# Attention with a soft mixture of experts on one core: local products over 128 keys instead of 64, paced transfers, four PSUM tiles for the output

## The chip, the cores and the metric

The kernel runs on one core of a Trainium2 chip. Its time is the device time of one execution, in microseconds (us), and the kernel before was run three times: 454.8, 461.24 and 464.32 us, median 461.24 us. The engines of the core work in parallel, each on its own queue of instructions in order: TensorE (PE; its weight loads stand as PEld), VectorE (DVE), ScalarE (ACT), GpSimd (POOL) and SyncE (SP), which here issues the transfers (DMA) between device memory and SBUF. Matrix products land in PSUM, eight banks of 512 fp32 values per partition.

## The reference

Eight batches of eight heads, 576 positions, head width 64; then a soft mixture of eight experts with four slots each over all 4608 tokens:

```python
scores = (q @ k.T) / sqrt(64), causal;  a = softmax(scores);  local = a @ v
q_p = phi(q)                                   # elu(x) + 1
mem_out = (q_p @ M_prev) / (q_p @ z_prev + 1e-6)
x = g * mem_out + (1 - g) * local              # g = sigmoid(beta), per head
logits = x @ phi                               # 4608 x 32
d = softmax over the tokens;  slot_input = d.T @ x
h = relu(slot_input[e] @ w1[e]);  slot_out[e] = h @ w2[e]      # 512 -> 1024 -> 512
c = softmax over the slots;  result = c @ slot_out
```

All of it is fp32. An fp32 product stands in the profile as two matmuls with a weight load each; the scores use three fp32r products of split operands.

## The kernel before, in words

**Units.** The attention is cut in 32 units `n` (a batch and a pair of heads; the two heads `h` lie on partitions 0 to 63 and 64 to 127). In a unit the last 512 queries are four blocks `i` of 128 queries, which see the first 192, 320, 448 and 576 keys. The first 64 queries of all units are done apart, in 16 small units ("a" operations). Nine groups `g` of tokens then run through the dispatch softmax ("x" operations), with a running maximum.

**Steps of a unit.** `ldq` and `ldv` load q and k, and v with `M` and `z`; `qhi`, `qlo`, `khi`, `klo` split q and k (POOL); `s` makes scores in PSUM (L367, L376); `mx` masks them and takes the row minimum (DVE, L394); `ex` takes the exponential (ACT, L401); `t` transposes the probabilities in blocks of 64 keys x 128 (two heads side by side; L404) and `te` copies them to SBUF (L283 on ACT, L286 on DVE); `av` multiplies with v (L433); `m` multiplies phi(q) with `M` and `z` (L442) into the same PSUM tile; `dn`, `mu`, `ad` normalise and add (L447, L454, L471). Each product of `av` is over 64 keys of one head for 64 queries, so TensorE works as four tiles of 64x64, and block `i` takes 8i+10 products (88 per unit). `pace` and its tiny copies do not exist yet.

**Order.** `SEQ` is a written table of some 2100 operations; `pin` ties every engine's instructions to that order. The digit behind a colon picks which of four PSUM tiles (two banks each) an operation gets. `EV` says which engine does a copy. `WORD` says where each of the 64 weight tiles of 512 KB is kept: with '' in space of its own, otherwise in a buffer that is free by then. Weight tiles that `WORD` does not hold are loaded in the last phase over used ones.

**Last phase.** `f1`, `f1t`, `f2` are the experts' layers. `comb(dh, g)` makes the output of a group, half the columns at a time: twice two products of 32 slots (L874) into a PSUM tile of two banks (three such tiles rotate), ACT scaling one pair (L880), DVE the other (L877), then a store of 512 KB.

Of the kernel before, what the change touches and what calls it, by code (L numbers as in the profile page):

```python
# [20 lines left out]
VM = 585 + 65  # L21
AU = 256 + 130 + 130
CW = 256 + S + 64
# [3 lines left out]
gate@0 la@0 la@1 ldq@1 ldv@1 as@0:0 ap1@0 aexp@0:1 amx.0@0 amx.1@0 aex.0@0 aphi@0 aex.1@0 at@0:1 as@1:0 ate@0 amx.0@1  # L27
aav@0:1 amx.1@1 am@0 aex.0@1 qhi@0 qp1@0 khi@0 la@2 adn@0 aex.1@1 qlo@0 qexp@0:0 klo@0 at@1:2 ate@1 amu@0 qhi@1 qphi@0
qp1@1 s.2@0:1 khi@1 qlo@1 aad@0 qexp@1:0 s.3@0:2 klo@1 mx.2.1@0 ldq@2 s.10@0:3 qphi@1 ex.2.1@0 ap1@1 mx.3a.1@0 s.2@1:0
mx.1.0@0 mx.3b.1@0 ex.1.0@0 mx.0.1@0 ldq@3 mx.1.1@0 ex.3.1@0 mx.0.0@0 ex.0.1@0 mx.3a.0@0 s.3@1:3 ex.0.0@0 ex.1.1@0  # L30
qhi@2 mx.2.0@1 aexp@1:2 khi@2 mx.3a.1@1 ex.2.0@1 qlo@2 aphi@1 mx.3b.1@1 t.C@0:2 mx.3a.0@1 ex.3.1@1 mx.3b.0@0 te.CX@0
s.10@1:3 klo@2 mx.3b.0@1 mx.2.1@1 te.CY@0 mx.2.0@0 ex.3.0@1 aav@1:0 am@1 as@2:2 mx.0.1@1 ex.2.1@1 qhi@3 av.1@0:1 la@3
amx.0@2 mx.1.0@1 aex.0@2 khi@3 ex.0.1@1 m.0@0 mx.1.1@1 ex.1.0@1 av.0@0 mx.0.0@1 qlo@3 ex.1.1@1 amx.1@2 s.10@2:3 dn.0@0
ex.0.0@1 aex.1@2 adn@1 ex.2.0@0 mu.0@0 at@2:2 klo@3 ex.3.0@0 amu@1 t.C@1:1 ate@2 mx.0.1@2 t.B@0:2 mx.1.0@2 ad.0@0
te.CY@1 mx.0.0@2 s.10@3:0 mx.1.1@2 te.BX@0 aad@1 te.CX@1 te.BY@0 t.A@0:3 ap1@2 mx.0.1@3 aexp@2:2 s.2@2:1 mx.1.0@3
te.AY@0 aphi@2 mx.0.0@3 te.AX@0 s.3@2:2 mx.1.1@3 mx.2.1@2 av.2@0:0 mx.3a.1@2 w@0 m.1@0 mx.3a.0@2 aav@2:3 am@2 av.3@0
qp1@2 mx.3b.1@2 mx.3b.0@2 la@4 adn@2 ap1@3 qexp@2:2 mx.2.0@2 amu@2 as@3:1 ldq@4 ldv@2 dn.1@0 av.1@1:3 aad@2 amx.0@3
mu.1@0 aex.0@3 m.0@1 av.0@1 amx.1@3 ex.1.0@2 ad.1@0 qphi@2 ex.0.0@2 t.B@1:1 aexp@3:0 dn.0@1 ex.0.1@2 x3.0@0:2 ex.1.1@2
mu.0@1 te.BX@1 aphi@3 te.BY@1 t.C@2:3 ad.0@1 x3e.0@0 aex.1@3 t.A@1:0 ex.2.1@2 qhi@4 te.CX@2 at@3:2 te.CY@2 s.2@3:1
khi@4 te.AX@1 te.AY@1 qlo@4 ate@3 ex.3.1@2 s.3@3:3 mx.2.1@3 ex.3.0@2 w@1 av.2@1:2 mx.2.0@3 ex.2.0@2 klo@4 mx.3a.1@3  # L40
m.1@1 aav@3:0 mx.3a.0@3 am@3 av.3@1 la@5 qp1@3 mx.3b.1@3 adn@3 ap1@4 mx.3b.0@3 qexp@3:3 amu@3 as@4:1 ldv@3 dn.1@1
av.1@2:0 aad@3 ldq@5 amx.0@4 amx.1@4 aex.0@4 mu.1@1 aexp@4:1 m.0@2 aex.1@4 av.0@2 aphi@4 ex.1.0@3 ad.1@1 qphi@3 at@4:1
# [36 lines left out]
mx.0.0@11 te.AY@9 qlo@12 s.3@11:1 mx.2.0@11 ex.2.1@10 av.2@9:3 ex.3.0@10 mx.2.1@11 klo@12 mx.3a.1@11 m.1@9 aav@11:2
mx.3a.0@11 am@11 av.3@9 la@13 qp1@11 mx.3b.1@11 adn@11 ap1@12 mx.3b.0@11 qexp@11:1 amu@11 as@12:0 ldv@11 dn.1@9  # L80
av.1@10:2 aad@11 ldq@13 amx.0@12 mu.1@9 aex.0@12 m.0@10 av.0@10 amx.1@12 ex.0.0@11 ad.1@9 qphi@11 ex.1.0@11 x4@1:0
aexp@12:3 dn.0@10 ex.0.1@11 aphi@12 aex.1@12 ex.1.1@11 mu.0@10 at@12:3 t.B@10:1 ex.2.0@11 x4a@1 ad.0@10 ate@12
t.C@11:2 w@11 ex.3.1@11 te.BX@10 s.10@12:3 te.BY@10 te.CX@11 t.A@10:0 qhi@13 te.CY@11 mx.1.0@12 s.2@12:1 khi@13
ex.2.1@11 mx.0.1@12 mx.1.1@12 te.AY@10 qlo@13 mx.0.0@12 s.3@12:2 te.AX@10 mx.2.0@12 ex.3.0@11 x3.1@2:3 mx.2.1@12
# [148 lines left out]
def tile_attn_soft_moe(ctx, tc, qk, vm, au, beta, phi, w1, w2, cst, out):  # L233
# [21 lines left out]
    psD = tc.alloc_tile_pool(name="psD", bufs=1, space=PSUM)  # L255
    ATT = (psD,)

    mk = fix.tile([128, 1152], F32, name="mk")
    maskq, mask2 = mk[:, 0:S], mk[:, S:S + 64]
    ph = fix.tile([128, NP, 32], F32, name="ph")  # L260
    gt = fix.tile([128, NP, 2, 4], F32, name="gt")
# [715 lines left out]
```

## Time and profile before

| what | value |
|---|---|
| median of three runs | 461.24 us (454.8 to 464.32) |
| the profiled execution | 462.31 us, of which span 460.4 us |
| busy: PE, DVE, ACT, POOL | 376.2, 308.9, 278.5, 198.3 us |
| attention with pipeline full, 22 to 386 us | PE 301.3 of 364 us |
| last phase, 398 to 460 us | 62 us |

Busy time is the union of an engine's instructions; TensorE's are pipelined, so its busy time is not work at its peak. The chain of waits follows the run back from its end. "issue" names idle time for which the profile shows no other engine or transfer as the cause. All durations below are from the one profiled execution.

### The profile page before, as it was taken

What the parts mean: (1) busy time and instruction counts of PE and PEld (TensorE: products, weight loads), DVE (VectorE), ACT (ScalarE), POOL (GpSimd) and SP (SyncE); (2) the same over time, 40 slices, a digit from 0 to 9 for tenths busy, and PEclk for the clock granted to TensorE, in tenths of its full rate; (3) what the DMA queues carried; (4) which work ended last, traced back from release to release, by engine and by line L of the source; (5) the groups of instructions that cost most, each with busy time, mean ns of one, the idle gap of its engine ahead of it and who ended that gap; (6) DMA issues with size and microseconds to landing.
All of it is one profiled execution on the core that took longest, in us unless ns stands there. A gap on an engine that the chain in (4) does not pass through costs nothing.

```text
span 460.4 us, 24149 instructions
## 1 busy us (share of the span) xinstructions
PE 376.2 (82%) x10675; PEld 304.1 (66%) x10675; DVE 308.9 (67%) x1148; ACT 278.5 (60%) x603; POOL 198.3 (43%) x255
## 2 busy tenths in 40 slices
PE   7698878886879787988798888989988865899882
PEld 3587767766867776777687777878778654435441
DVE  2888778776857787777768768788877632441432
ACT  2677776766867677566766777677667541030542
POOL 0656553755454456555636645665555201000000
PEclk9689999999989999899989999999999897599996
DMA  6424444454454445345324322241356476199978
GB/s 248 117 75 151 154 147 156 143 195 152 149 151 149 147 153 172 130 121 170 131 94 160 127 80 82 81 141 52 115 184 215 171 268 237 53 383 417 339 249 304
DMA packets 30953, 77.79 MB, mean 169 GB/s; under 512 B 2817, under 2 KB 12289, under 8 KB 30849
## 3 DMA queue, kind: packets, MB, share of 16 engines
q1 hardware_dynamic: 30560, 76.16, 48.5%
q8 instruction: 84, 1.38, 1.2%
q14 instruction: 21, 0.16, 0.1%
q10 hardware_dynamic: 288, 0.08, 0.1%
HBM read 66.80 MB, written 9.44 MB: 166 GB/s over the span
## 4 chain that ended last, share of the span: by engine, by line
PE 69%; issue 14%; DVE 9%; ACT 7%; POOLq 0%; POOL 0%; DVEq 0%; ACTq 0%
PE psD L433 22%; PE psD L367 14%; PE psD L404 11%; ACT at L283 3%; PE pf L800 3%; PE psD L442 3%; PE pf L817 3%; DVE at L286 3%; PE pp L874 2%; PE psD L578 2%; PE psD L622 2%; PE psD L300 2%; ACT p L401 1%; PE psD L376 1%; DVE p L394 1%
## 5 line engine op out<-in xcount | busy, mean ns | idle before, releaser
L433 PE MATMUL psD<-vm,at 64*64 64x65 f32 x5632 | 125.7, 223 | 32.6 <-issue 30.4
L401 ACT ACTIVATE p<-p,nm 128x448 f32<-128x448 f32 (+3 forms) x256 | 143.7, 613 | 3.7 <-DVE nm L394 3.7
L433 PEld LDWEIGHTS psD<-vm,at 64*64 64x64 f32 x5632 | 114.2, 136 | 44.9 <-issue 38.4
L394 DVE CUSTOM_DVE_ANT_0 p<-psD,mk 128x448 f32<-128x448 f32 (+3 forms) x256 | 124.2, 536 | 24.4 <-PE psD L367 12.1
L367 PE MATMUL psD<-K,X 64*128 64x320 f32 (+3 forms) x768 | 103.4, 374 | 13.8 <-issue 9.0
L283 ACT COPY at<-psD 128x512 f32<-128x512 f32 (+1 forms) x143 | 74.0, 560 | 54.6 <-DVE at L286 38.3
L471 POOL TENSOR_TENSOR x<-w 128x256 f32<-128x256 f32 x64 | 46.8, 731 | 98.0 <-DVE w L454 96.0
L367 PEld LDWEIGHTS psD<-K,X 64*128 64x128 f32 x768 | 72.7, 203 | 18.2 <-issue 12.4
L404 PE MATMUL psD<-cs,p 64*128 64x64 f32 x1408 | 68.4, 230 | 10.1 <-issue 4.5
L404 PEld LDWEIGHTS psD<-cs,p 64*128 64x128 f32 x1408 | 59.5, 142 | 20.8 <-issue 9.7
L454 DVE TENSOR_TENSOR w<-psD,R 128x512 f32<-128x512 f32 x64 | 44.0, 687 | 2.6
L347 POOL TENSOR_TENSOR K<-qk,K 128x576 fp32r<-128x576 f32 x31 | 44.5, 1434 | 0.0
L339 POOL TENSOR_TENSOR X<-qk,X 128x512 fp32r<-128x512 f32 x31 | 39.7, 1282 | 3.4 <-DVE aR L539 3.4
L447 DVE SCALAR_TENSOR_TENSOR R<-psD,gt 128x8 f32<-128x8 f32 x64 | 10.5, 164 | 44.7 <-PE psD L433 44.4
L442 PE MATMUL psD<-vm,f 64*64 64x65 f32 x1024 | 37.9, 226 | 2.3 <-issue 2.3
L351 POOL TENSOR_SCALAR f<-qk 128x512 f32<-128x512 f32 x32 | 20.3, 634 | 45.3 <-PE psD L442 40.0
L286 DVE COPY at<-psD 128x512 f32<-128x512 f32 (+1 forms) x49 | 30.3, 622 | 12.4 <-ACT at L283 9.9
L355 ACT ACTIVATE psD<-qk 128x512 f32<-128x512 f32 x32 | 19.2, 602 | 24.1 <-DVE nm L394 9.8
L442 PEld LDWEIGHTS psD<-vm,f 64*64 64x64 f32 x1024 | 30.5, 136 | 2.7 <-issue 2.6
L288 POOL TENSOR_SCALAR X<-qk 128x512 fp32r<-128x512 f32 x30 | 18.6, 619 | 28.4 <-DMA qk<-in_qk_dram 26.6
L394 DVE DVE_READ_ACCUMULATOR2_ANT nm<- 128x1 f32 x320 | 26.7, 83 | 0.0
L283 ACT COPY xd<-psD 128x512 f32<-128x512 f32 x27 | 15.8, 586 | 14.2 <-PE psD L404 14.2
(168 smaller groups left out, 476.5 us busy)
## 6 DMA issues: line engine op xcount, KB each, us to landing
w<-in_w_dram SPq DMA_DIRECT2D x42, 512.0 KB, 6.4
qk<-in_qk_dram SPq DMA_DIRECT2D x32, 544.0 KB, 4.4
vm<-in_vm_dram SPq DMA_DIRECT2D x32, 325.0 KB, 3.6
au<-in_au_dram SPq DMA_DIRECT2D x16, 258.0 KB, 2.8
p<-in_w_dram SPq DMA_DIRECT2D x6, 512.0 KB, 6.0
out_dram<-w SPq DMA_DIRECT2D x4, 512.0 KB, 3.3
out_dram<-p SPq DMA_DIRECT2D x3, 512.0 KB, 4.7
xa<-in_w_dram SPq DMA_DIRECT2D x2, 512.0 KB, 4.2
```

Source lines behind the costliest of these rows:

```text
L283: nc.scalar.copy(o, i)
L286: nc.vector.tensor_copy(out=o, in_=i)
L339: ALU_ENG[ev("qlo", n)].tensor_tensor(out=x[:, 1], in0=st[n]["q"], in1=x[:, 0].bitcast(F32), op=ALU.subtract)
L347: ALU_ENG[ev("klo", n)].tensor_tensor(out=x[:, 1], in0=st[n]["k"], in1=x[:, 0].bitcast(F32), op=ALU.subtract)
L367: nc.tensor.matmul(ps[:, h, c:c + k1 - k0], s["X"][ROW[h], x, 128 * i:128 * i + 128], s["K"][ROW[h], y, k0:k1], start=(x, y) == (0, 0), st ...
L394: nc.vector.tensor_tensor_reduce(out=s["p", i][:, k0 // 64:k1 // 64, h], in0=s["s", u][:, h, c:c + k1 - k0].rearrange("a (k x) -> a k x", ...
L401: nc.scalar.activation(p, p, AF.Exp, scale=-1.0, bias=s["nm"][:, 2 * i + h:2 * i + h + 1])
L404: nc.tensor.transpose(out=o, in_=i, identity=ident[ROW[r], ROW[r]])
L433: nc.tensor.matmul(s["u", u][64 * c:64 * c + 64, h, 65 * x + 130:65 * x + 195], atq[i][ROW[h]] if last else at_block(i, k)[ROW[h], c], s[" ...
L442: nc.tensor.matmul(s["u", u][64 * c:64 * c + 64, h, 65 * x:65 * x + 65], s["f"][ROW[h], o:o + 64], s["m"][ROW[h]], start=True, stop=True)
L454: nc.vector.tensor_tensor(out=w, in0=s["u", u][:, :, 0:260].rearrange("a h (x d) -> a h x d", d=65)[:, :, :, 0:64], in1=s["R", u].rearrang ...
L471: ALU_ENG[ev(f"ad.{u}", n)].tensor_tensor(out=o, in0=w[:, :, 0:2], in1=w[:, :, 2:4], op=ALU.add)
```

## The change

1. **`av` over 128 keys.** The probabilities are kept per head with the keys in one run (the second head's keys reversed), transposed in blocks of 128 keys of one head, and `v` is loaded with 128 keys on the partitions. A product now covers 128 keys and 64 queries (128 partitions x 64 columns, half of the array's columns). The last 64 keys of a block, which only 64 queries see, stay products on 64x64 tiles; they move into `m`. Per unit 88 products become 40 on column halves and 8 on 64x64 tiles. One PSUM tile thus collects products of both tilings.
2. **Transfers.** q and k are loaded apart; `v` with its second layout is 845 columns wide instead of 650, the mask 1216 instead of 640. Before most transfers ScalarE makes a copy of one element of the buffer (`pace`, `wload`), so that the transfer cannot start before ScalarE has come to that place: 104 copies to `tick` and 22 into fresh weight tiles, 126 in all.
3. **Last phase.** `psF` and `psP` become four tiles of one bank and two of two banks; `comb` makes its four products one after the other into four banks; the remaining `f2` of the second half is spread over the nine `comb(0, g)`. Twenty weight tiles instead of 19 are loaded in this phase.
4. **A new `SEQ`, `EV` and `WORD`.** Copies `te` and `x3e` on ACT rise from 170 to 185.

```diff
+    def pace(t):
+        if paced[0]:
+            nc.scalar.copy(tick, t[0:1, 0:1])
+
+    def op_ldk(n):
+        if n > 1:
+            pace(st[n - 2]["k"])
...
+        nc.sync.dma_start(out=st[n]["k"], in_=qk[n, :, 512:QK])
     def op_ldq(n):
-        t = st[n]["qk"] = dbl.tile([128, QK], F32, name="qk")
-        st[n]["q"], st[n]["k"] = t[:, 0:512], t[:, 512:QK]
-        nc.sync.dma_start(out=t, in_=qk[n])
+        if n > 1:
+            pace(st[n - 2]["q"])
+        nc.sync.dma_start(out=st[n]["q"], in_=qk[n, :, 0:512])
...
     def op_av(n, i):
...
-        for k in range(2 * i + 3):
-            last = k == 2 * i + 2
+        for k in range(i + 1):
             for h in range(2):
-                for c in range(last, 2):
-                    nc.tensor.matmul(s["u", u][64 * c:64 * c + 64, h, 65 * x + 130:65 * x + 195], atq[i][ROW[h]] if last else at_block(i, k)[ROW[h], c], s["v"][ROW[h], k],
-                                     start=k == 0, stop=k == 2 * i + 1 + c)
+                for c in range(2):
+                    nc.tensor.matmul(s["u", u][64 * c:64 * c + 64, h, 65 * x + 130:65 * x + 195], at_block(i, 2 * k + h)[:, c], s["v"][:, k, h],
+                                     start=first and k == 0, stop=False)
     def op_m(n, u):
...
+            for h in range(2):
+                nc.tensor.matmul(s["u", u][64:128, h, 65 * x + 130:65 * x + 195], atq[i][ROW[h]], s["vr"][ROW[h], i], start=False, stop=x == 1)
...
     def wload(x, pool, name, half=None):
+        if paced[0] and pool is wres:
+            nc.scalar.copy(t[0:1, 0:1], one)
...
-    psF = ctx.enter_context(tc.tile_pool(name="psF", bufs=2, space=PSUM, reuse_waits="tile"))
-    psP = ctx.enter_context(tc.tile_pool(name="psP", bufs=3, space=PSUM, reuse_waits="tile"))
+    psF = ctx.enter_context(tc.tile_pool(name="psF", bufs=1, space=PSUM, reuse_waits="tile"))
+    psP = ctx.enter_context(tc.tile_pool(name="psP", bufs=2, space=PSUM, reuse_waits="tile"))
+    SINGLE = ["pa0", "pa1", "pf0", "pf1"]
...
     def comb(dh, g):
-        for half in range(2):
-            ps = psP.tile([128, 2, 512], F32, name="pp")
-            for v2 in range(2):
...
+        ps = [single(3 + dh), single(3 + dh), psP.tile([128, 2, 512], F32, name="pp")]
+        s2 = [ps[0], ps[1], ps[2][:, 0], ps[2][:, 1]]
+        for u in range(4):
+            r = slice(32 * u, 32 * u + 32)
+            nc.tensor.matmul(s2[u][:, 0:256], cT[r, GO.index(g), :], so[r, dh], start=True, stop=True)
...
+    left = [(e, f, c) for e in range(2) for f in range(2) for c in range(4)][4:]
     for i, g in enumerate(GO):
         comb(0, g)
-        if i == 4:
-            f2(1, 0, 1)
-    f2(1, 1, 0)
-    f2(1, 1, 1)
+        for e, f, c in [left.pop(0) for _ in range(2 if i % 3 == 2 else 1)]:
+            f2(1, e, f, (c,))
```

TensorE's order in one unit of the attention, before (`vm` is v, `M` and `z`; `at` the transposed probabilities; `f` phi(q); `x16` counts products):

```order
L404 MATMUL psD_6048<-cs,p_5770 128x64 x14
L433 MATMUL psD_6067<-vm,at 64x65 x26
L442 MATMUL psD_6067<-vm,f 64x65 x8
L433 MATMUL psD_6067<-vm,at 64x65 x34
L433 MATMUL psD_6146<-vm,at 64x65 x18
L442 MATMUL psD_6146<-vm,f 64x65 x8
L433 MATMUL psD_6146<-vm,at 64x65 x10
L578 MATMUL psD_6190<-xd,ph 32x128 x16
```

and in the changed kernel (L461 is `av` on column halves, L471 and L473 are `m` with the last keys, on 64x64 tiles):

```order
L402 MATMUL psD_4551<-qk 128x64 x2
L461 MATMUL psD_4567<-vm,at 64x65 x12
L471 MATMUL psD_4567<-vm,f 64x65 x4
L473 MATMUL psD_4567<-vm,at 64x65 x2
L471 MATMUL psD_4567<-vm,f 64x65 x4
L473 MATMUL psD_4567<-vm,at 64x65 x2
L461 MATMUL psD_4603<-vm,at 64x65 x28
L471 MATMUL psD_4603<-vm,f 64x65 x4
L473 MATMUL psD_4603<-vm,at 64x65 x2
L471 MATMUL psD_4603<-vm,f 64x65 x4
L473 MATMUL psD_4603<-vm,at 64x65 x2
L393 MATMUL psD_4664<-K,X 128x512 x6
```

Before, the unit's products stand in one run on 64x64 tiles; now each half of them passes from one tiling to another. Counted over the attention, the order changes tiling 89 times before and 232 times now.

ScalarE's order in the middle of the attention, in the changed kernel (L336 and L677 are the copies of one element; L426 is `ex`, L290 `te` and `x3e`, L380 and L520 exponentials for phi):

```order
L290 COPY xd<-psD_1545 128x2x4x64
L336 COPY tick<-qk 1x1
L426 ACTIVATE p_1492<-p_1492,nm 128x448
L520 ACTIVATE psD_1593<-au 128x128
L677 COPY w_1651<-one 1x1
L290 COPY at<-psD_1619 128x512
L290 COPY at<-psD_1636 128x384
L290 COPY at<-psD_1636 128x512
L336 COPY tick<-vm 1x1
L380 ACTIVATE psD_1700<-qk 128x512
```

The rows L336 and L677 are new; nothing like them stands in the order before.

TensorE in the last phase of the changed kernel, in the middle of the nine `comb(0, g)` (L921 is `comb`, L864 `f2`); before, the products of five groups stand together as `L874 MATMUL pp<-w,cT 128x256 x16` and the like, with `f2` between and behind:

```order
L921 MATMUL pf_8212<-w,cT 128x256
L921 MATMUL pa_8213<-w,cT 128x256
L921 MATMUL pp<-w,cT 128x256 x2
L864 MATMUL pf_8110<-w_8008,x 32x256
L864 MATMUL pf_8110<-w_8010,x 32x256
L864 MATMUL pf_8110<-w_8012,x 32x256
L864 MATMUL pf_8110<-w_8014,x 32x256
```

Here a piece of `f2` (four to eight products) follows every group of four output products.

## Rows read from the trace of the kernel before

**Rows 1.** The page: span, busy time of the engines, chain by engine
```profile
span 460.4 us, 24149 instructions
...
PE 376.2 (82%) x10675; PEld 304.1 (66%) x10675; DVE 308.9 (67%) x1148; ACT 278.5 (60%) x603; POOL 198.3 (43%) x255
...
PE 69%; issue 14%; DVE 9%; ACT 7%; POOLq 0%; POOL 0%; DVEq 0%; ACTq 0%
```
**Rows 2.** Busy time in stretches: us, then busy (instructions) per engine, clock, DMA
```profile
69.43:72.77 3.34, 3.33 (x126) 3.13 (x127) 2.64 (x13) 1.06 (x4) 1.44 (x3) 1.00 0.56 157
22.00:386.00 364.00, 301.34 (x9920) 265.57 (x9920) 271.82 (x1054) 247.12 (x529) 189.43 (x241) 0.97 0.44 144
```
**Rows 3.** Waits of TensorE: for whom, us in total, times, longest
```profile
PE psD L433 <- issue: 30.4, 27, 2.8
PE psD L367 <- issue: 9.0, 8, 2.4
PE psD L404 <- issue: 5.2, 6, 1.6
```
**Rows 4.** DMA queues of the page: packets, MB, share
```profile
q8 instruction: 84, 1.38, 1.2%
```
**Rows 5.** Chain of waits: start us, us, what, matmuls
```profile
56.44 1.63 PE psD L433 x97
...
67.63 1.80 issue
...
72.77 0.75 issue
...
74.68 1.21 PE psD L404 x30
...
131.36 1.05 PE psD L578 x32
...
396.01 1.88 PE psD L722 x8
...
418.27 5.36 PE pf L817 x96
```
**Rows 6.** Timeline of TensorE where the tiling changes, at 71.4 us
```profile
71.18 0.22 PE L433 MATMUL psD<-vm,at 64*64 64x65 f32 x1
71.33 0.27 PE L404 MATMUL psD<-cs,p 64*128 64x64 f32 x2
```
**Rows 7.** Groups by line and form: tiling, shapes, count, busy us, mean ns
```profile
L433 PE MATMUL psD<-vm,at 64*64 64x65 f32 x5632 | 125.7, 223 | 32.6 <-issue 30.4 <-DVE at L286 0.9 <-ACT at L283 0.5
...
L578 PEld LDWEIGHTS psD<-xd,ph 128*32 128x32 f32 x288 | 7.5, 111 | 5.3 <-issue 3.0 <-ACT xd L283 1.7
```
**Rows 8.** Busy time while L722 ran: columns as in rows 2
```profile
396.01:397.89 1.88, 1.88 (x9) 1.88 (x10) 0.24 (x2) 0.00 (x0) 0.00 (x0) 0.50 0.02 4
```
**Rows 9.** Groups of copies and small activations on ScalarE
```profile
L283 ACT COPY at<-psD 128x512 f32<-128x512 f32 x102 | 57.2, 591 | 23.1 <-DVE at L286 16.7 <-PE psD L404 6.1
...
L595 ACT ACTIVATE al<-mrun,mrun 128x1 f32<-128x1 f32 x9 | 2.5, 283 | 0.0
...
L283 ACT COPY aat<-psD 128x128 f32<-128x128 f32 x9 | 2.3, 260 | 3.7 <-PE psD L404 3.7
```
**Rows 10.** Timeline of the start: first small unit, first scores
```profile
7.56 0.28 ACT L488 ACTIVATE psD<-au 128x128 f32<-128x128 f32 x1 [3.12 <-DMA au<-in_au_dram]
...
14.29 1.49 PE L367 MATMUL psD<-K,X 64*128 64x448 f32 x6 [1.32 <-DVE aw L546]
```
**Rows 11.** Busy time in stretches of the last phase: columns as in rows 2
```profile
412.00:424.00 12.00, 12.00 (x186) 5.79 (x184) 2.64 (x5) 1.18 (x2) 0.00 (x0) 1.00 1.03 418
442.00:446.00 4.00, 3.00 (x26) 1.36 (x25) 1.39 (x2) 2.57 (x7) 0.00 (x0) 1.00 0.48 165
446.00:454.00 8.00, 5.71 (x48) 2.92 (x48) 4.84 (x7) 5.01 (x13) 0.00 (x0) 0.94 1.06 374
```
**Rows 12.** Timeline of the last phase: output products of the second half
```profile
444.56 1.43 PE L874 MATMUL pp<-w,cT 32*128 32x256 f32 x12 [0.51 <-ACT X L880]
```

More of the change, by code (lines that the diff above doesn't have):

```diff
@@ L20 @@
 QK = 512 + S
-VM = 585 + 65
+VM = 780 + 65
 AU = 256 + 130 + 130
-CW = 256 + S + 64
+CW = 256 + 2 * S + 64
 AG = 8
 SEQ = """
[L27 to L30, printed above, removed]
@@ L256, in tile_attn_soft_moe @@
     ATT = (psD,)
-    mk = fix.tile([128, 1152], F32, name="mk")
-    maskq, mask2 = mk[:, 0:S], mk[:, S:S + 64]
+    mk = fix.tile([128, 2 * S + 64], F32, name="mk")
+    maskq, mask2 = mk[:, 0:2 * S], mk[:, 2 * S:2 * S + 64]
     ph = fix.tile([128, NP, 32], F32, name="ph")
@@ L272, in tile_attn_soft_moe @@
     auf = fix.tile([128, 2 * AU], F32, name="au")
+    qkf = fix.tile([128, 2 * QK], F32, name="qk")
     vmf = fix.tile([128, 2 * VM], F32, name="vm")
@@ L303, in setup @@
         warm()
-        nc.sync.dma_start(out=mk[:, 0:S + 64], in_=cst[:, 256:CW])
+        nc.sync.dma_start(out=mk, in_=cst[:, 256:CW])
         nc.sync.dma_start(out=cs, in_=cst[:, 0:256])
@@ L318, in op_gate @@
         nc.vector.reciprocal(out=l, in_=l)
+    paced = [False]
+    tick = const.tile([1, 1], F32, name="tick")
+    def pace(t):
[4 more added lines that the diff above has]
+            pace(st[n - 2]["k"])
+        t = qkf[:, QK * (n % 2):QK * (n % 2) + QK]
+        st[n]["q"], st[n]["k"] = t[:, 0:512], t[:, 512:QK]
+        nc.sync.dma_start(out=st[n]["k"], in_=qk[n, :, 512:QK])
     def op_ldq(n):
[L323 to L325 removed]
+        if n > 1:
+            pace(st[n - 2]["q"])
+        nc.sync.dma_start(out=st[n]["q"], in_=qk[n, :, 0:512])
     def op_ldv(n):
         t = vmf[:, VM * (n % 2):VM * (n % 2) + VM]
[L329 to L330 removed]
+        pace(t)
+        st[n]["v"] = t[:, 0:520].rearrange("a (k h x) -> a k h x", k=4, h=2)
+        st[n]["vr"] = t[:, 520:780].rearrange("a (i x) -> a i x", i=4)
+        st[n]["m"] = t[:, 780:VM]
         nc.sync.dma_start(out=t, in_=vm[n])
@@ L408, in op_t @@
         ps = s["t", t] = bank()
-        full = {"A": [(3, k) for k in range(8)], "B": [(2, k) for k in range(6)], "C": [(1, k) for k in range(4)] + [(0, k) for k in range(2)]}[t]
-        rest = {"A": [], "B": [(3, 8), (2, 6)], "C": [(1, 4), (0, 2)]}[t]
-        for x, (i, k) in enumerate(full + rest):
+        full = {"A": [(3, kb, h) for kb in range(4) for h in range(2)],
+                "B": [(2, kb, h) for kb in range(3) for h in range(2)],
+                "C": [(1, kb, h) for kb in range(2) for h in range(2)] + [(0, 0, h) for h in range(2)]}[t]
+        for x, (i, kb, h) in enumerate(full):
             for r in range(2):
-                if r or x < len(full):
-                    turn(ps[:, r, 64 * x:64 * x + 64], s["p", i][ROW[r], k].rearrange("a h x -> a (h x)"), r)
+                turn(ps[:, r, 64 * x:64 * x + 64], s["p", i][ROW[r], h, (128 * kb, 64 + 128 * (i - kb))[h]:][:, 0:128], r)
+        for x, i in {"A": (), "B": ((6, 3), (7, 2)), "C": ((6, 1), (7, 0))}[t]:
+            turn(ps[:, 1, 64 * x:64 * x + 64], s["p", i][ROW[1]].rearrange("a h x -> a (h x)")[:, LEN[i] - 64:LEN[i] + 64], 1)
     TE = {"AX": (0, 512), "AY": (512, 512), "BX": (1024, 384), "BY": (1408, 512), "CX": (1920, 384), "CY": (2304, 512)}
@@ L438, in op_m @@
         for x in range(2):
+            i = 2 * u + x
             for h in range(2):
                 for c in range(2):
-                    o = 256 * u + 128 * x + 64 * c
-                    nc.tensor.matmul(s["u", u][64 * c:64 * c + 64, h, 65 * x:65 * x + 65], s["f"][ROW[h], o:o + 64], s["m"][ROW[h]], start=True, stop=True)
+                    o = 128 * i + 64 * c
+                    nc.tensor.matmul(s["u", u][64 * c:64 * c + 64, h, 65 * x:65 * x + 65], s["f"][ROW[h], o:o + 64], s["m"][ROW[h]], start=False, stop=x == 1 and c == 0)
+            for h in range(2):
+                nc.tensor.matmul(s["u", u][64:128, h, 65 * x + 130:65 * x + 195], atq[i][ROW[h]], s["vr"][ROW[h], i], start=False, stop=x == 1)
     def op_dn(n, u):
@@ L479, in op_la @@
         s["v"], s["m"] = (t[:, 256 + 130 * i:386 + 130 * i].rearrange("a (m x) -> a m x", m=2) for i in range(2))
+        pace(t)
         nc.sync.dma_start(out=t, in_=au[n])
@@ L796, in f1 @@
     def f1(eg, f):
-        ps = psF.tile([128, 512], F32, name="pf")
+        ps = pf()
         for c in range(4):
@@ L813, in f2 @@
         if dh not in po:
-            po[dh] = psF.tile([128, 512], F32, name="pf")
+            po[dh] = pf()
         for c in cs_:
@@ L863, in g2 @@
     def g2(dh):
-        pm = psP.tile([128, 2, 512], F32, name="pp")[:, 0]
+        pm = single(2)
         nc.tensor.matmul(pm[:, 0:256], sel, ogs[:, dh], start=True, stop=True)
@@ L869, in comb @@
         o = wtile(*stage[NG * dh + g]).rearrange("a (c x) -> a c x", c=4)
-        for half in range(2):
-            ps = psP.tile([128, 2, 512], F32, name="pp")
-            for v2 in range(2):
-                r = slice(64 * half + 32 * v2, 64 * half + 32 * v2 + 32)
-                nc.tensor.matmul(ps[:, v2, 0:256], cT[r, GO.index(g), :], so[r, dh], start=True, stop=True)
-            r = s36[:, GO.index(g), half]
-            if half:
-                nc.vector.tensor_tensor(out=o[:, 2:4, :], in0=ps[:, :, 0:256], in1=r.rearrange("a (j o) -> a j o", o=1).broadcast_to([128, 2, 256]), op=ALU.mult)
-            else:
-                for v2 in range(2):
-                    nc.scalar.activation(o[:, v2, :], ps[:, v2, 0:256], AF.Copy, scale=r[:, v2:v2 + 1])
+        ps = [single(3 + dh), single(3 + dh), psP.tile([128, 2, 512], F32, name="pp")]
[3 more added lines that the diff above has]
+            nc.tensor.matmul(s2[u][:, 0:256], cT[r, GO.index(g), :], so[r, dh], start=True, stop=True)
+        r = s36[:, GO.index(g)].rearrange("a r j -> a (r j)")
+        for u in range(2):
+            nc.scalar.activation(o[:, u, :], s2[u][:, 0:256], AF.Copy, scale=r[:, u:u + 1])
+        nc.vector.tensor_tensor(out=o[:, 2:4, :], in0=ps[2][:, :, 0:256], in1=r[:, 2:4].rearrange("a (j o) -> a j o", o=1).broadcast_to([128, 2, 256]), op=ALU.mult)
         d = slice(256 * dh, 256 * dh + 256)
@@ L958 @@
     mz = np.concatenate([M, z[..., None]], axis=3).reshape(B * NP, 128, D + 1)
-    a["vm"] = c(np.concatenate([vt.reshape(B * NP, 128, 585), mz], axis=2))
+    vp = np.concatenate([v, np.full((B, H, S, 1), 1000.0, v.dtype)], axis=3).reshape(B * NP, 2, S, D + 1)
+    vk = vp[:, :, :512].reshape(B * NP, 2, 4, 128, D + 1).transpose(0, 3, 2, 1, 4)
+    vk = np.stack([vk[:, :, :, 0], vk[:, ::-1, :, 1]], axis=3).reshape(B * NP, 128, 520)
+    vr = vp.reshape(B * NP, 2, 9, 64, D + 1)[:, :, 2::2].transpose(0, 1, 3, 2, 4)
+    vr = np.stack([vr[:, 0], vr[:, 1, ::-1]], axis=1).reshape(B * NP, 128, 260)
+    a["vm"] = c(np.concatenate([vk, vr, mz], axis=2))
     def two(t):
```

418 lines of the change are left out of this document (218 added, 200 removed).

## The prediction

> **What bounds the kernel now.** I read the page first, for who works most; then the stretches, for where; then the waits, the queues and the chain, for why the busiest engine stands still. TensorE is busy longest and holds 69% of the chain, with another 14% put down to "issue" [rows 1]. In the 364 us in which the attention pipeline is full it is busy 301.3 us, against 271.8 for DVE and 247.1 for ACT [rows 2]. So it is the bound there, and 63 us of the stretch are its own idle time.
>
> Most of that idle time has one cause. Three groups of waits on "issue" hold 30.4 + 9.0 + 5.2 = 44.6 us in 41 stops [rows 3]. The chain shows two neighbours, at 67.63 and 72.77 us [rows 5]; between them TensorE ran 126 matmuls and 127 weight loads, 253 instructions [rows 2]. The instruction queue moved 1.38 MB in 84 packets, 16.4 KB each [rows 4], and the kernel has 2 x 10675 TensorE instructions [rows 1], that is 254 to a packet. So the engine stops at the seams between packets of its own program: the next packet is not there when the last one is used up. The stretch holds 19840 / 254 = 78 seams, and a seam costs 44.6 / 78 = 0.57 us on average, up to 2.8 us at worst.
>
> **The products.** Removed: 5632 matmuls (2816 products) on 64x64 tiles [rows 7]. The chain passes 97 of them in 1.63 us [rows 5], 16.8 ns each, so 94.6 us. Added: 512 for the last keys at the same rate, 8.6 us, and 2560 on column halves, which the trace before does not show. Lower end: column tiles of 128 partitions that stream 256 columns take 5.36 us / 96 = 55.8 ns with four tiles at work [rows 5], 223 ns per tile and 0.87 ns per column; 65 columns on two tiles are then 28.3 ns, 72.4 us in all. Upper end: transposes with two tiles at work, 1.21 us / 30 = 40.3 ns [rows 5], 103 us. I take the row with the same weights and the same 65 columns, at half as many tiles: 2 x 16.8 = 33.6 ns, 86.0 us. **Net 0.0 us**, bounds -13.6 and +17.
>
> **Changes of tiling.** From the last 64x64 product to the first transpose 0.15 us pass, start to start [rows 6], where 0.017 us would be the pace: 0.13 us per change. There are 143 more of them, 18.6 us. About one sixth of the stretch is idle anyway (63 of 364 us), and a change that falls there is free: **+15 us**. Bounds: nothing if all hide in stops, 143 x 0.223 us = 32 us if each waits a matmul's full mean duration [rows 7].
>
> **The seams.** 2560 matmuls fewer are 5120 instructions, 20 seams fewer: 20 x 0.57 = 11 us at least. The remaining 58 get shorter, since what is queued when a packet is ordered lasts longer at 33.6 ns a matmul than at 16.8. I take 0.33 us for each, 19 us instead of 44.6: **-26 us**, bounds -11 and -40 (stops nearly gone).
>
> **ScalarE.** A copy of 512 columns takes 591 ns, of 128 columns 260 [rows 9]; the line through them meets zero columns at 150 ns, and the smallest activation, with two operands per partition, takes 283 [rows 9]. 126 one-element copies are 19 us, at most 36. Fifteen more large copies add 9 us. ACT would be at 275 us in the stretch, still below TensorE's, so I cost it at nothing. The cover is TensorE's time; if it goes, these 28 us are the price (a rival below). DVE loses ten `te`, some 6 us, and is not the bound.
>
> **Transfers.** 325 KB per unit become 422 KB, 3.2 MB in all, and there is room beside 144 GB/s, since the last phase moves 418 [rows 2, 11]. What queues behind a transfer that waits for a copy on ACT is every later load, SP being one queue; the loads are ordered a good part of a unit ahead of their readers, so I cost it at nothing, and the price if they come late is in the same rival.
>
> **Start.** The first scores begin at 14.29 us, behind two small units whose data landed at 7.56 [rows 10]. The new order splits k and q of unit 0 first and scores right behind the first small unit; but that unit's data stand behind 0.4 MB more of mask and v. **-2 us**, bounds -5 and +3.
>
> **Last phase.** It is half bound by transfers: 418 GB/s while weights come [rows 11], 374 at the end, with a hole of 165 between 442 and 446 us, when `f2`, `g1`, `g2` stand between the last store of one half and the first of the other [rows 11]. Output products run 12 in 1.43 us, 119 ns each [rows 12], at two banks; four banks can halve that. But spread `f2` adds a change of tiling before and behind every group, 18 x 0.13 = 2.3 us and more, one more weight tile is 0.5 MB at 418 GB/s, 1.3 us, and the stores cannot end sooner than their bandwidth lets them. What can be won is the hole: **-2 us**, bounds -5 and +2.
>
> **Sum.** The profiled execution took 462.3 us: 462.3 + 0 + 15 - 26 - 2 - 2 = 447.3. That execution is 0.2% above the median of the three runs, which changes nothing. Forecast: **447 us**.
>
> **Rivals.**
>
> *The weight loads come into the open, slower.* On four tiles a load on one tile can hide behind the products of three others; on two column halves only one other is at work. For it: L722, where the array is one tile and nothing else can run, takes 1.88 us / 8 = 235 ns for only 32 moving columns [rows 5], at a clock of 0.50, the lower level of 1.2 GHz [rows 8]. Half of that for full clock and half again for 64 weight columns is 59 ns. Against it: L578, on four column tiles, passes 32 in 1.05 us, 32.8 ns for 128 columns [rows 5], although each of its weight loads lasts 111 ns [rows 7]. At 59 ns the products cost 65 us more, and the seams would be slow enough to hide wholly (-40): 462.3 + 65 + 15 - 40 - 4 = 498. It decides from (471 - 447) / 2560 matmuls above my price, 43 ns, only just beyond the transposes.
>
> The Trainium skill bears on this rival ("TensorE: Matmul & The Clock Gate", Part 3): weight loads overlap with running matmuls only where the row group differs. Column halves have all row groups in common, so by that rule no load would hide, and the time would be this rival's 498 us. The row of L578, whose column tiles share their row groups as well, speaks against the rule. That is why it has the smaller chance.
>
> *ACT's cover goes, no change.* ACT with 28 us more comes to 275 of what would be 345 us, each copy in the middle of the in-order queue that TensorE's four PSUM tiles wait for. If half of the 28 us shows, the time is 461. For it: that is 80% in a queue that cannot reorder. Against it: 44.6 of TensorE's 63 idle us are seams, so little of its waiting today is for others.
>
> *The seams vanish and the products stream at their lower end, more gain.* 462.3 - 13.6 + 15 - 40 - 4 = 420; a half of both gives 433.
>
> **Chances and range.** The forecast (437 to 457) gets 0.50, the exposed loads 0.15, ACT's cover 0.20, the greater gain 0.15. Two per cent is about what repeated runs of this kernel can tell from no change; around 461.24 that is 452 to 470.5. Faster by over 2%: two thirds of the forecast (0.35), all of the greater gain (0.15), a little of ACT's case (0.04) make 0.54. Slower: the exposed loads nearly whole, with a little of ACT's case, 0.15. Within: 0.31. The range goes from 430, which leaves out half of the greater gain (0.07), to 468, which leaves out the exposed loads (0.13).
>
> **What would show it.** Products: start to start of L461 matmuls near 34 ns; over 43 and the first rival holds. Changes of tiling: 0.15 us from an L461 to an L471 matmul; more of it than 0.2 would make the forecast too low. Seams: 64 packets on the instruction queue instead of 84, and waits of TensorE on "issue" near 19 us instead of 45; if these stay at 35 or more, the step that fails is the pace at the seam. ACT: one-element copies near 0.15 us, and TensorE's waits for ACT and DVE no longer than now; if they grow by more than 10 us, the second rival holds. Last phase: no hole near the middle of the stores. The forecast would be wrong altogether if TensorE's busy time in the full stretch, changes of tiling included, grew by more than its idle time shrank.

## The result and the profile after

The changed kernel takes **411.73 us** (median of four runs, 411.19 to 412.82), the kernel before 462.46 us beside it: a ratio of 0.900, 95% interval 0.892 to 0.907. I had forecast 447 us, 430 to 468. The sign was right; the gain is 50.7 us where I expected 15, and the time lies below the range. Medians and ranges, here and below, are of all runs, ratios and intervals of the fast runs alone (a run over 1.5% above the shortest of its kernel counts as slow).

The profiled execution took 411.43 us. Its page has these answers to [rows 1, 4]:

```profile
span 409.7 us, 19301 instructions
...
PE 371.6 (91%) x8115; PEld 301.3 (74%) x8115; DVE 303.2 (74%) x1136; ACT 295.6 (72%) x741; POOL 198.0 (48%) x255
...
q8 instruction: 64, 1.05, 1.1%
...
PE 49%; ACT 24%; DVE 16%; issue 4%; DMA 3%; SPq 1%; POOLq 0%; POOL 0%; DVEq 0%; ACTq 0%
```

The span fell by 50.7 us, TensorE's busy time by only 4.6 (376.2 to 371.6). The other 46.1 us are its own idle time, 84.2 before and 38.1 now. So what was won is not work but standing still, and the waits say which. TensorE's waits after, the two largest and the two on issue (for whom, us in total, times, longest), beside [rows 3]:

```profile
PE psD L429 <- ACT p L426: 4.4, 10, 1.0
PE psD L461 <- DVE at L293: 2.0, 4, 0.9
...
PE psD L461 <- issue: 0.9, 1, 0.9
...
PE psD L429 <- issue: 0.6, 3, 0.2
```

The waits on issue were 44.6 us in the three groups of [rows 3], 50.2 with the four smaller groups; now they are 1.5. Waits for anything else went from 24.7 us to 23.2, all groups added. The stretch with the pipeline full (columns as in [rows 2]) and two stretches of the last phase:

```profile
22.00:336.00 314.00, 299.04 (x7326) 263.35 (x7323) 265.13 (x1037) 263.00 (x661) 189.67 (x241) 1.00 0.57 174
359.00:371.00 12.00, 11.52 (x174) 5.45 (x170) 3.12 (x5) 1.94 (x4) 0.00 (x0) 1.00 1.03 409
387.50:391.50 4.00, 2.84 (x38) 1.44 (x34) 1.31 (x3) 1.45 (x4) 0.00 (x0) 1.00 0.98 280
```

From 22 us to the last product, TensorE is busy 299 of 314 us; before it was 301 of 364. The hole in the middle of the last phase is shallower (280 GB/s where there were 165), but the phase itself, from the first `f1` matmul to the end of the span, takes 62.1 us against 62.2: 347.5 to 409.7 us.

The new products in the chain of waits, and the change of tiling in the timeline of TensorE:

```profile
191.96 1.78 PE psD L461 x56
193.74 0.39 PE psD L429 x8
```
```profile
181.58 0.86 PE L461 MATMUL psD<-vm,at 128*64 128x65 f32 x23
182.37 0.38 PE L471 MATMUL psD<-vm,f 64*64 64x65 f32 x9
```

56 in 1.78 us are 31.8 ns each; I had taken 33.6. From the last L461 of the second fence (182.22) to the first L471 (182.37) 0.15 us pass, as I had taken. The copies of one element and the first scores, beside [rows 9, 10]:

```profile
L336 ACT COPY tick<-qk 1x1 f32<-1x1 f32 x60 | 10.5, 176 | 0.0
...
L677 ACT COPY w<-one 1x1 f32<-1x1 f32 x22 | 3.9, 177 | 0.0
```
```profile
10.97 0.49 PE L393 MATMUL psD<-K,X 64*128 64x512 f32 x2 [0.18 <-ACT X L290]
```

So the prices were nearly right, and one size was badly off: the seams. The rest is about why.

### The profile page after: what moved, and what is told of

It is laid out like the page before. It is cut to its first block, busy times and chain, and to the rows that moved or that the text cites. A ratio compares the mean times of both kernels' runs of the same rounds, so it can differ in the third digit from the quotient of the medians.

```text
span 409.7 us, 19301 instructions
## 1 busy us (share of the span) xinstructions
PE 371.6 (91%) x8115; PEld 301.3 (74%) x8115; DVE 303.2 (74%) x1136; ACT 295.6 (72%) x741; POOL 198.0 (48%) x255
## 4 chain that ended last, share of the span: by engine, by line
PE 49%; ACT 24%; DVE 16%; issue 4%; DMA 3%; SPq 1%; POOLq 0%; POOL 0%; DVEq 0%; ACTq 0%
ACT p L426 13%; PE psD L461 11%; PE psD L429 9%; PE psD L393 9%; DVE p L420 7%; ACT at L290 6%; PE pf L847 4%; PE pf L864 4%; PE psD L471 4%; DVE at L293 3%; DMA qk<-in_qk_dram 2%; ACT xd L290 2%; PE pa L921 2%; DVE w L485 1%; PE psD L654 1%
## 5 line engine op out<-in xcount | busy, mean ns | idle before, releaser
L426 ACT ACTIVATE p<-p,nm 128x576 f32<-128x576 f32 (+3 forms) x256 | 144.1, 608 | 12.4 <-DVE nm L420 11.9
L461 PE MATMUL psD<-vm,at 128*64 128x65 f32 x2560 | 89.8, 224 | 4.7 <-DVE at L293 2.0
L393 PE MATMUL psD<-K,X 64*128 64x320 f32 (+3 forms) x768 | 91.8, 355 | 2.0 <-DVE at L293 0.5
L290 ACT COPY at<-psD 128x512 f32<-128x512 f32 (+1 forms) x153 | 77.7, 551 | 20.3 <-PE psD L429 17.8
L461 PEld LDWEIGHTS psD<-vm,at 128*64 128x64 f32 x2560 | 80.8, 138 | 14.0 <-issue 3.2
L393 PEld LDWEIGHTS psD<-K,X 64*128 64x128 f32 x768 | 63.5, 188 | 8.4 <-DVE at L293 1.0
L372 POOL TENSOR_TENSOR K<-qk,K 128x576 fp32r<-128x576 f32 x30 | 42.6, 1421 | 2.2
L471 PE MATMUL psD<-vm,f 64*64 64x65 f32 x1024 | 36.8, 233 | 0.0
L293 DVE COPY at<-psD 128x384 f32<-128x384 f32 (+1 forms) x39 | 23.9, 621 | 15.8 <-ACT at L290 15.2
L295 POOL TENSOR_SCALAR K<-qk 128x576 fp32r<-128x576 f32 x30 | 20.2, 673 | 29.4 <-PE psD L393 24.0
L473 PE MATMUL psD<-vm,at 64*64 64x65 f32 x512 | 33.5, 218 | 0.0
L471 PEld LDWEIGHTS psD<-vm,f 64*64 64x64 f32 x1024 | 28.2, 132 | 5.7 <-issue 1.7
L473 PEld LDWEIGHTS psD<-vm,at 64*64 64x64 f32 x512 | 26.4, 135 | 0.0
L290 ACT COPY xd<-psD 128x512 f32<-128x512 f32 x32 | 18.3, 575 | 9.2 <-PE psD L429 9.0
```

The costliest lines, as they stand in the source:

```text
L290: nc.scalar.copy(o, i)
L372: ALU_ENG[ev("klo", n)].tensor_tensor(out=x[:, 1], in0=st[n]["k"], in1=x[:, 0].bitcast(F32), op=ALU.subtract)
L393: nc.tensor.matmul(ps[:, h, c:c + k1 - k0], s["X"][ROW[h], x, 128 * i:128 * i + 128], s["K"][ROW[h], y, o + k0:o + k1], start=(x, y) == (0 ...
L426: nc.scalar.activation(p, p, AF.Exp, scale=-1.0, bias=s["nm"][:, 2 * i + h:2 * i + h + 1])
L461: nc.tensor.matmul(s["u", u][64 * c:64 * c + 64, h, 65 * x + 130:65 * x + 195], at_block(i, 2 * k + h)[:, c], s["v"][:, k, h], start=first ...
L471: nc.tensor.matmul(s["u", u][64 * c:64 * c + 64, h, 65 * x:65 * x + 65], s["f"][ROW[h], o:o + 64], s["m"][ROW[h]], start=False, stop=x == ...
```

## The theories

Before the experiments I looked once more at two neighbouring stops of the kernel before. Its chain of waits there (start us, us, what):

```profile
220.52 1.10 issue
221.62 0.39 PE psD L433 x10
...
222.43 1.40 PE psD L433 x86
223.83 1.14 issue
```

and its busy time between the two stops:

```profile
221.62:223.83 2.21, 2.20 (x127) 2.08 (x128) 0.47 (x4) 2.00 (x6) 1.31 (x2) 1.00 0.03 7
```

TensorE runs 255 instructions in 2.21 us and then stands for 1.1 us: from stop to stop 3.31 us. No two of the 84 instruction packets start closer together than 3.30 us in this trace (3.20 in any trace shown here). This gives the **supply theory**: packets come no faster than one in 3.3 us, so the engine stops only where 127 matmuls take less, that is under 26 ns each. The **count theory** is the one of my forecast: a seam has its price, fewer seams cost less. The **order theory** says that the new order and the pacing removed the waits.

## The experiments

**`after_oldprod`: the new order with the old products.** Keys, mask, `t`, `av` and `m` as before, all else of the change kept.

```diff
-        for k in range(i + 1):
-            for h in range(2):
-                for c in range(2):
-                    nc.tensor.matmul(..., at_block(i, 2 * k + h)[:, c], s["v"][:, k, h], ...)
+        for k in range(2 * i + 3):
+            last = k == 2 * i + 2
+            for h in range(2):
+                for c in range(last, 2):
+                    nc.tensor.matmul(..., atq[i][ROW[h]] if last else at_block(i, k)[ROW[h], c], s["v"][ROW[h], k], ...)
```

> The changed kernel with its first part undone: keys, mask and products as before (64*64 tiles, 5632 product matmuls), but the new order, the pacing by ScalarE, the split loads and the new last phase kept. Supply theory: 127 product matmuls at 16.8 ns are used up in 2.1 us, under the 3.3 us of a packet, so 84 packets and 35 to 50 us of waits on issue come back; products cost 7 us more and some 140 tiling changes go (-15): 412 + 42 + 7 - 15 = 446 us, 435 to 456. Order theory: the waits stay away, 412 + 7 - 15 = 404. Count theory: 20 seams x 0.57 = +11, so 415.

Measured 448.3 us (442.7 to 452.5), 0.963 of before [0.953, 0.974], and 31 us over the change even in its shortest run. The chain and the waits of its profiled run (451.6 us):

```profile
211.41 1.55 PE psD L458 x89
212.96 1.58 issue
```
```profile
PE psD L458 <- issue: 28.7, 20, 4.0
PE psD L467 <- issue: 5.0, 4, 1.5
```

Products at 17.4 ns, 84 packets, 42.6 us of waits on issue with all groups. The new order does not keep them away: order theory out, and count theory's 415 us too. The trace has 158 changes of tiling before `f1`, so 79 of the change's 237 go with the old products, and not the 140 that I expected; the others belong to the new order.

**`before_double`: the old order and count, slower products.** 130 moving columns instead of 65.

```diff
-  ... h, 65 * x + 130:65 * x + 195], ..., s["v"][ROW[h], k],
+  ... h, 65 * x + 130:65 * x + 260], ..., s["t2"][ROW[h], 65 * k:65 * k + 130],
```

> The kernel before with 130 instead of 65 moving columns in each local product (the second half is the next block of v, so the sums are not the reference's); as many instructions, same order. The f2 rows give 0.22 ns per column on four tiles, so a product matmul goes from 16.8 to about 31 ns and the products cost 5632 x 14 = 79 us more. Supply theory: a packet then lasts 3.9 us, the waits on issue fall to under 10, 462 + 79 - 42 = 499 us, 488 to 510. Count and order theory: the waits stay, 541 us, over 530.

Measured 477.1 us (475.4 to 479.7), ratio 1.036 [1.028, 1.044]. Its page's instruction queue, its chain and its waits:

```profile
q8 instruction: 84, 1.38, 1.2%
```
```profile
225.28 2.83 PE psD L433 x96
```
```profile
PE psD L433 <- issue: 5.8, 5, 2.2
...
PE psD L404 <- issue: 0.5, 2, 0.3
```

The same 84 packets in the same order, twice the columns, and 44 of the 50 us of waits are gone. A product takes 29.5 ns, 3.7 us for 127. This is the sharpest of the tests: nothing but the pace was changed. The time is 11 us below the supply theory's range: TensorE's busy time rose by 61 us (376.2 to 437.0), not by 79. The slope that I took from `f2` is too steep for these tiles: at the paces of the chain the products cost 5632 x (29.5 - 16.8) = 72 us more. Most of the rest would be the clock, which in this run falls once between 22 us and the last product, and six times before (below). 462.6 + 61 - 44 = 480 is near what was measured.

**`before_half`: half of that.** 97 columns; the edit is the same with 97 for 130.

> The kernel before with 97 instead of 65 moving columns in each local product (the extra 32 are from the next block of v, so the sums are not the reference's); same instructions, same order. With 130 columns a product matmul took 29 ns, with 65 16.8, so 97 should take about 23 ns, and 127 of them 2.9 us, still under the 3.3 us at which packets follow each other. Supply theory: the waits on issue fall by (23 - 16.8) x 127 = 0.8 us per packet full of products, from 50 to about 15 to 25 us, and the time hardly moves: 462 + 5632 x 6.2 = 35, less 25 to 35: 462 to 472. Count theory: waits stay at 50 us, 497.

Measured 462.1 us over ten runs (457.8 to 468.9), ratio 1.005 [1.001, 1.010]: half as many columns again for about 2 us. Its chain, and its largest wait on issue:

```profile
244.43 2.09 PE psD L433 x96
```
```profile
PE psD L433 <- issue: 17.0, 19, 3.3
```

21.8 ns each; 25.6 us of waits on issue with all groups, in a profiled execution of 468.9 us. Here slower work filled time in which the engine would have stood. The kernels of both layouts side by side:

| kernel | ns per product matmul, chain | 127 of them | waits on issue |
|---|---|---|---|
| before | 16.8 | 2.1 us | 50.2 us |
| after_oldprod | 17.4 | 2.2 us | 42.6 us |
| before_half | 21.8 | 2.8 us | 25.6 us |
| before_double | 29.5 | 3.7 us | 6.3 us |
| after | 31.8 | 4.0 us | 1.5 us |

The waits shrink as the products slow down, as the supply theory has it, but its line of 3.3 us is not sharp. At 3.7 us for 127 products 6.3 us of waits remain. In the trace of before, 36.6 of the 50.2 us fall on stops whose packet started over 3.8 us after the packet ahead of it, so the shortest spacing did not hold it up. What all 116 stops in the first four kernels of the table share is another time: each ended 2.2 to 2.9 us after the start of the newest packet. A stop is what is left of that time once TensorE has used up the instructions that it still had; in a few, the longest of 4.0 us in `after_oldprod` among them, the packet started only when TensorE had already run out. A whole packet of products at 16.8 ns lasts 2.1 us and cannot cover it; at 31.8 ns, as an estimate, a little over half to three quarters of a packet can. What decides when a packet starts is not shown.

**`before_wide`: the old order, half as many instructions.** Both column halves in one matmul on a tile of 64 rows and 128 columns.

```diff
-                for c in range(last, 2):
-                    nc.tensor.matmul(s["u", u][64 * c:64 * c + 64, h, ...], atq[i][ROW[h]] if last else at_block(i, k)[ROW[h], c], s["v"][ROW[h], k], ...)
+                nc.tensor.matmul(s["u", u][:, h, ...], at_block(i, k)[ROW[h]], s["v"][ROW[h], k], ...)
```

(`te` writes its blocks so that a block's 128 columns lie together; `m` likewise.)

> The kernel before, in its own order and with its own key layout, but every local product and every product with the memory on 64*128 tiles (both column halves in one matmul): 3584 matmuls where there were 6656. Supply theory: a packet of about 254 TensorE instructions never follows the last one sooner than 3.3 us (the shortest spacing in the trace before), and the engine stops only where it uses a packet up faster. At the transposes' 36 ns a packet of 127 matmuls lasts 4.6 us, so the waits on issue fall from 50 us to under 8; products cost 3584 x 36 = 129 us instead of 94.6 + 17.9; some tiling changes go (-6): 462 - 43 + 16 - 6 = 429 us, 418 to 440. Count theory (my forecast's: every seam costs 0.57 us): 24 seams fewer, -14, so about 458. Order theory (the new order and pacing removed the waits): nothing of it is here, so 465 to 475.

Measured 486.9 us (482.7 to 495.1), ratio 1.054 [1.044, 1.064]: slower, and my price was wrong. Its chain:

```profile
214.19 3.13 PE psD L434 x56
...
218.43 0.37 PE psD L406 x12
```

A product takes 55.9 ns, a transpose of the same tile shape 31. I had priced the products with the transposes. 3584 x 55.9 = 200 us are 88 more than before. TensorE has no wait on issue left in its trace (a profiled execution of 495.1 us), as the supply theory has it, but here that is bought too dear.

**`after_oldorder`: the new products in the old order.** `SEQ`, tile numbers and `EV` of before, no pacing, `m` behind its pair of `av`. Against the list of before, cut:

```diff
-ldq@2 ... m.0@0 ... av.0@0
+ldk@2 ldq@2 ... av.0@0 m.0@0
```

> The changed kernel (column halves, fixed qk buffers, new last phase) with the order list, tile numbers and copy assignment of the kernel before; k and q loads stand where the one load stood, no pacing, and a memory product stands right behind its unit's second local product. Supply theory: the waits on issue stay under 5 us, since the pace of the products is that of the change. With the old products the order and pacing were worth 462.6 - 448.3 = 14 us; 8 of that was waits on issue, so 412 + 6 = 418 us, at most 426. Order theory, as far as it still stands: 30 us or more of waits come back, over 440.

Measured 417.5 us (415.9 to 418.8), 0.910 [0.906, 0.915]. Its first scores in the timeline, and its largest wait on issue:

```profile
15.09 1.49 PE L237 MATMUL psD<-K,X 64*128 64x448 f32 x6 [1.41 <-DVE aw L422]
```
```profile
PE psD L273 <- issue: 1.8, 1, 1.8
```

The waits stay away in the old order. Order and pacing together are worth 5.8 us, and 4.1 of it is the start (15.09 against 10.97): from the first scores to the first `f1` matmul both kernels take 336.5 to 336.6 us.

**`after_unpaced`: without the copies of one element.**

```diff
-        paced[0] = sl == "+"
```

> The changed kernel without the 126 one-element copies on ScalarE (loads then wait for their buffers only). If the copies cost ScalarE time that TensorE feels: 2 to 6 us faster than 411.7. If they keep loads out of the way of others: slower by 2 us or more. My forecast costed them at nothing: 410 to 413.

Measured 410.5 us (408.8 to 412.6), 0.891 [0.884, 0.899]: no difference from the change that these runs can tell. ACT's busy time on its page fell by 9.4 us:

```profile
PE 373.1 (91%) x8115; PEld 303.5 (74%) x8115; DVE 303.5 (74%) x1136; ACT 286.2 (70%) x615; POOL 197.7 (48%) x255
```

**`after_split`: 128 more changes of tiling.**

```diff
+        if first:
+            rest(n, i, False)      # last-key products of this block, behind its av
```

> The changed kernel with the last-key products of the first of each pair of query blocks moved from behind the pair to between its two blocks: the same instructions, 128 more changes between 128*64 and 64*64 tiles. By the forecast's price, 0.13 us each and on the path: +16.6, 428 us. If such changes hide in idle time now: 412 to 415, since 18 us of idle time are left. If the drain is dearer behind products on column halves (a whole matmul of 0.22 us): +28, 440.

Measured 422.6 us (421.1 to 425.4), 0.922 [0.915, 0.929]: 10.9 us over the change, between the two cases that I had set out. The trace has 365 changes before `f1` where there were 237, so 0.085 us each. Its chain shows the split pair:

```profile
185.84 0.85 PE psD L461 x24
186.69 0.26 PE psD L471 x4
186.95 1.08 PE psD L461 x32
```

Here L471 is the moved product. About two thirds of a change's 0.13 us shows in the end. TensorE's busy time rises by the full price, 16.4 us (371.6 to 388.0), 0.128 for each of the 128; its idle time falls by 4.0 us, from 38.1 to 34.1.

**`after_oldtail`: the old last phase.** `psF`, `psP`, `comb` and the placing of `f2` as before.

```diff
-        ps = [single(3 + dh), single(3 + dh), psP.tile([128, 2, 512], F32, name="pp")]
+        for half in range(2):
+            ps = psP.tile([128, 2, 512], F32, name="pp")
```

> The changed kernel with the last phase of the kernel before (two pairs of banks for the output products, f2 of the second half in whole blocks). The forecast gave the new last phase 2 us (bounds -5 and +2): 413 to 417. By the traces, f1's first matmul to the end of the span takes 62.1 us before and 62.2 after: 410 to 413.

Measured 412.5 us (410.8 to 414.9), 0.900 [0.895, 0.905]: the same. In its trace `f1` starts at 346.5 us:

```profile
346.50:410.50 64.00, 50.66 (x584) 22.81 (x584) 19.75 (x33) 19.60 (x46) 0.00 (x0) 0.90 0.87 313
```

64.0 us for the phase, 1.9 more than in the change. But `after_unpaced` and `after_split`, which have the new phase, take 62.9 and 63.1, so the phases cannot be told apart by this. Both load 20 weight tiles there; the kernel before loads 19 and takes 62.2. That the four banks win what I gave them and the twentieth weight tile takes it back would fit, but no run shows it.

## Why the prediction was wrong, point by point

| term | forecast | measured |
|---|---|---|
| products | 0 (-13.6 to +17) | 94.6 to about 90 us: -4.5 |
| changes of tiling | +15 (0 to +32) | 143 x 0.085 = +12 |
| seams | **-26** (-11 to -40) | **-48.7** |
| ScalarE's copies | 0 | 0 |
| start | -2 | first scores 3.3 us earlier |
| last phase | -2 | 0 |
| clock | not in the sum | about -8 (an estimate, below) |

**The step that failed** is "The remaining 58 get shorter ... I take 0.33 us for each, 19 us instead of 44.6". The direction was right and I had even named the reason, that the queue lasts longer at 33.6 ns than at 16.8. But I scaled an average instead of asking what a seam costs at a given pace. The answer was in the trace of before: two stops 3.31 us apart with 2.21 us of work between them. A packet of 127 products at my own 33.6 ns lasts 4.3 us, over 3.3; its seam costs next to nothing, as the runs show. With that, the same sum gives 462.3 + 15 - 45 to 50 - 4 = about 425. I also took only the three groups of [rows 3]; the four smaller ones hold another 5.6 us, and they went as well. Of what 425 still lacks to 411.7, products and changes of tiling that came cheaper than I priced them make 7 to 8 us, and a term that I had put at nothing, the clock, some 8.

**Products.** 31.8 ns in the chain, 30.3 as the mean of 2,495 starts: 2560 x 30.3 = 77.6 us, and the 512 last-key products, mixed with those of `m`, take about 24 ns, 12.5 us. The row that I chose (same weights, same columns, half the tiles) was the right one. **Changes of tiling**: the duration was right (0.15 us start to start), and the share that shows, two thirds rather than five sixths, was near.

**The weight loads do not come into the open.** On column halves a tile's turn takes 2 x 31.8 = 64 ns, though each of its weight loads lasts 138 ns and each matmul 224:

```profile
L461 PE MATMUL psD<-vm,at 128*64 128x65 f32 x2560 | 89.8, 224 | 4.7 <-DVE at L293 2.0 <-ACT at L290 1.3 <-issue 0.9
L461 PEld LDWEIGHTS psD<-vm,at 128*64 128x64 f32 x2560 | 80.8, 138 | 14.0 <-issue 3.2 <-DVE at L293 2.5 <-DVE nm L420 1.2
```

The rule of the Trainium skill by which loads overlap only across row groups ("TensorE: Matmul & The Clock Gate", Part 3) would have made this kernel slower. The trace disagrees with it here, as L578 [rows 7] did.

**ACT's cover** held. The one-element copies take 22 us together (176 ns each, where I had 150), but without them ACT's busy time falls by only 9.4. ACT is busy 263 of the 314 us, near the 275 that I feared, and TensorE's waits for ACT and DVE went from 23.0 us to 20.8. That rival had the most chance after the forecast and nothing of it came. **The greater gain** came true in its first half: the seams vanished (-48.7 where it had -40), but the products came to -4.5 and not to its -13.6. It comes nearest of the cases: I priced it at 420 us and gave it 0.15, where the two rivals on the other side had 0.35 between them.

**The clock** stands in no term of the forecast, though [rows 2] give 0.97 for the full stretch before. In six spells between 22 and 386 us the granted clock stood at the lower of its two levels, 1.2 GHz. Here are two stops and a run of products from the chain of before, then the busy time in the two spells that came behind those stops, and the sum over all six:

```profile
361.99 2.00 issue
...
373.33 2.84 issue
...
378.81 1.07 PE psD L433 x32
```
```profile
364.23:367.65 3.42, 3.42 (x90) 2.64 (x88) 2.38 (x7) 0.00 (x0) 0.72 (x1) 0.50 0.63 197
377.89:381.30 3.41, 3.41 (x112) 3.29 (x110) 1.70 (x3) 1.06 (x2) 0.73 (x1) 0.50 0.72 201
sum 20.48, PE 20.48 PEld 18.75 DVE 11.78 ACT 11.00 POOL 10.18; mean PE 3.41 PEld 3.12 DVE 1.96 ACT 1.83 POOL 1.70
```

TensorE is busy in all of these 20.5 us. The 32 products take 33.4 ns each where they take 16.8 at the upper level; over all starts in the trace, transposes take 57 ns against 35. So the same work would need some 10 to 12 us at the upper level, and the spells cost about 8 us, an estimate. In the changed kernel the clock is 1.00 from 22 to 336 us, as its row in the section on the result shows. Over whole executions the mean granted clock was 0.928 to 0.951 in the runs of before beside the experiments, 0.963 to 0.966 in the four of the change and 0.966 to 0.970 in those of `before_double`. Four of the six falls came within 3 us behind a stop on issue of 1.4 to 2.8 us, one behind waits for DVE and ACT, one just after the start. In `after_oldprod` all four falls of the full stretch came right behind stops of 2.0 to 4.0 us; in `before_double`, nearly without stops, there is one at the start and no other. So most of this gain came with the stops, and no run separates the two.

The terms as measured, without the clock, add to -44.5 of 50.9 us between the two profiled executions, with 1.5 more in the other waits. The clock's 8 us cover the 5 that are left, and some more: the terms are not exact to a few us. Why an instruction packet takes 2.2 to 2.9 us from its start to its use, and what decides when it starts, stays open.

## What to carry to other kernels

Where a busy engine stops for "issue", set the time that it needs for one packet of its own instructions against the shortest spacing of those packets: here 254 instructions against 3.3 us. Well below that line, work on the instructions' speed is given back as stops, and larger, slower ones cost little: 65 to 97 columns, about 2 us. Above it nearly all stops are gone and not only a share of them: 6.3 and 1.5 us are left of 50. The line itself is not sharp, since some packets start late. Look at the granted clock behind each stop too: where it falls, the stop can cost more than its own length. Price a tile shape only with rows of the same kind of instruction: transposes and products of one shape differed by nearly two.

## What the runs showed of the hardware that I had not expected

- Moving columns for nothing: 65 to 97 per product, half as many again, changed the time of the kernel before by 0.5% [0.1%, 1.0%].
- A product on a tile of 64 rows and 128 columns takes 55.9 ns with two tiles at work, so 112 ns of a tile's time; with 64 weight columns a tile needs 64 to 67 (31.8 x 2, 16.8 x 4). Transposes of that tile shape, 62 (0.37 us / 12, two tiles). The Trainium skill ("TensorE: Matmul & The Clock Gate", "LDWEIGHTS (loading the stationary operand)") lets a weight load grow with its columns, from which an estimate is 53 ns for 64 and 107 for 128: that is like the products and unlike the transposes. The rows of the loads differ in the same way, though each lasts longer than the estimate: 136 ns for the products' 64 columns (L433), 195 for 128 (L434 in `before_wide`), but 142 for the 128 of the transposes (L404).
- The chain of waits of the changed kernel goes through ACT and DVE for 40% of the span while TensorE is busy for 91% of it: with the seams gone three engines are close together.
